# Delta attention, squared-ReLU layer and maxout layer on one core: due places and weights of the written-out schedule changed

## The chip, the cores and the metric

The kernel runs on one core of a Trainium2 chip. The metric is the device time of one execution in microseconds (us); smaller is better. TensorE (PE) multiplies matrices, its weight loads are listed apart as PEld; VectorE (DVE) and ScalarE (ACT) work on tiles, GpSimd (POOL) only fills memory here, and SyncE (SP) issues every DMA, one after the other.

## The reference

Three layers follow each other. The first is a delta-rule attention over 4 batches, 8 heads, 768 steps and head width 48:

```python
for t in range(S):
    kt, vt, bt = (k_n[:, :, t], v[:, :, t], beta[:, :, t, None])
    y[:, :, t] = np.einsum('bhd,bhde->bhe', q[:, :, t], state)
    v_old = np.einsum('bhde,bhd->bhe', state, kt)
    state = state + bt[:, :, :, None] * np.einsum('bhd,bhe->bhde', kt, vt - v_old)
...
h = x @ w_in; g = np.maximum(h, 0) ** 2; x = g @ w_out                     # 384 -> 2048 -> 384
h = np.maximum(np.maximum(x @ w1, x @ w2), x @ w3); return h @ w_out2      # 384 -> 768 -> 384
```

`k_n` is k divided by its norm. Layers two and three work on 3072 rows. The weights arrive as 64-bit floats.

## The kernel before

**Tiling.** The 768 steps are cut into six segments t = 0 to 5 of 128 steps, and each segment into two halves of 64. For each segment there are four pieces of attention work. `gram(t)` (line 499) transposes keys and queries on TensorE and multiplies them; ScalarE and VectorE (with the mask, tile W) move the products. `solve(t)` (line 568) inverts triangular 32x32 blocks on VectorE: a prologue, then 31 steps j of two instructions each (tiles tmp and T, line 621), then transposes (Tn, G) and small TensorE products between them (tiles Tn, G and L). `values(t)` scales v (tile vn). `chain(t)` (line 708) carries the state through the segment: removals (VectorE, tile R), updates (ScalarE, US), states (VectorE, US) and outputs (ScalarE, Y), each with TensorE products in two groups; `rows` (line 792) then issues ten small DMAs, xr<-Y, for each half. The chain needs the solve of its own segment and the state of the chain before it. `split` (line 827) cuts the outputs into a high and a low part, xh and xl.

**The first dense layer.** `moe1(t)` (line 872) works on the 512 rows of segment t in 16 feature blocks f. For each f, `hidden` does 9 matmuls of 512 columns from xh, xl, wih and wil, then squares on ScalarE (r, gh) and VectorE (gl), and `project` does 9 more with wo into three accumulators that stay for the whole segment. At t = 0 the weights of each f are loaded and converted from 64 bits: `load_in` and `load_out`, both by `load_w` (line 839), two ScalarE and seven VectorE instructions apiece, 32 such conversions. The converted wo is written to DRAM (wod<-wo) and streamed back for t > 0 (wo<-wod) into a ring of four buffers (line 426). There is one xh and one xl, so `split(t+1)` waits for the last `hidden` of t. At t = 0 the first eight blocks run in two halves.

**The maxout layer** follows in three planned stages: the rest of moe1 for t = 4 and 5 with the conversions of the maxout weights, then the maxout work.

**What sets the order.** Nothing is issued at once. Each instruction is recorded with a due place `pl.at` (in ticks; one feature block of moe1 is 6 ticks, a segment TICKS = 96) and a modelled cost, and `Planner.issue` writes out an order for all engines together (three calls: lines 996, 1070, 1084). It runs `forward` eight times (line 262): a list schedule in which each engine takes, among the instructions that are ready, the one with the smallest due place. After each round `backward` replaces all due places by the latest places that the schedule just made would allow. The round with the earliest modelled end is issued. So the due places in the code steer the first round, and the later ones through it. On TensorE the dense matmuls (float32r) and the attention's (float32) are two kinds; five weights decide when it goes from one kind to the other (lines 159 to 172): MIX and FULL are the planner's floors of work in a stretch below which it takes dense matmuls, STAY says how much more urgent dense work must be to end a group of attention work, URGENT how much more urgent attention work must be to break into dense work, and BURST how many microseconds of ready attention work break in without being urgent. HOLD (line 150) lets VectorE take an instruction that becomes ready up to so many microseconds after it is free.

**Due places** that the change touches: `solve(1, G1 - TICKS)` (line 979), `chain(t + 1, TICKS * t - CL)` and its values (lines 985, 986), `gram` and `solve` of t + 2 at TICKS * t - GL and 12 later (lines 988, 989), the streamed wo at SPL ticks ahead of its `project` (line 908), and the second half of the small products in solve(0), LATE ticks after the first (lines 664, 691). DEC, BOOST, G2 and the rest stay. chain(0) is due at -192 ticks, and the conversions of block f at 6f - 100 and 6f - 91 (3f in the halves).

Of the kernel before, what the change touches and what calls it, by code (L numbers as in the profile page):

```python
# [52 lines left out]
class Planner:  # L53
# [3 lines left out]

    MIX, FULL, STAY, BURST, URGENT = 4344, 6200, 5.0, 1.5, 5.0  # L60
    INTO, BACK = 0.09, 0.2
    HOLD = {"vector": 0.15}
    LAG = {"tensor": 0.2, "vector": 0.13, "scalar": 0.15, "gpsimd": 0.08, "sync": 0.0}

    def __init__(self, nc):
# [48 lines left out]
    def forward(self, at):  # L114
# [20 lines left out]
        while todo:  # L135
# [13 lines left out]
            r = ready.get(e, [])  # L149
            while r and r[0][0] <= t + self.HOLD.get(e, 0.0):  # L150
                when, n = heappop(r)
# [174 lines left out]
def kernel(  # L326
# [41 lines left out]
    GB = B // 2  # L368
    EPS = 1e-6

    GL, CL, G1, DEC, BOOST, SPL, CUT, HALF, G2, LATE, EARLY = 46, 20, -19, 100, 125, 23, 6, 8, -111, 88, 0
    TICKS = 6 * NF
    W_MIN, W_MAX = 2.0 ** -15, 122876.0

# [740 lines left out]
```

## Time and profile before

| what | value |
|---|---|
| median of three runs | 993.63 us (993.24 to 993.89) |
| the profiled execution | 994.74 us; its span from first to last instruction 992.6 us |
| PE busy | 918.2 us, 92% of the span |
| DVE busy | 581.6 us, 59% |
| ACT busy | 466.8 us, 47% |
| mean granted TensorE clock | 0.942 of full |

How to read it: a busy share is of the whole span, while each stretch has its own limit. The page cuts the span into 40 slices of 24.8 us and gives each engine one digit for each, the tenths in which it was busy, and PEclk the tenths of TensorE's full clock that were granted. TensorE knows two levels here, 2.4 GHz (9, 1.00) and 1.2 GHz (5, 0.5); values between them are slices with both. Matmuls overlap in the records, so a matmul's mean duration is longer than the distance between two starts.

### The profile page before, as it was taken

To read this page: it belongs to the slowest core of one execution; us is meant where nothing else is said; L and a number is where in the kernel's file an instruction comes from. 1 tells how busy PE (TensorE), PEld (TensorE's weight loads), DVE (VectorE), ACT (ScalarE), POOL (GpSimd) and SP (SyncE) were. 2 spreads that over 40 slices of the span, in tenths; PEclk is the share of its full clock that TensorE was granted. 3 is DMA by queue.
4 is the path that set the end of the run, shared out by engine and by line. 5 is a ranking of instruction groups with operands and counts; after the bars stand their busy time and mean duration, and the time that the engine had idled before them with its cause. 6 is when DMAs were issued, how large, how long until landed. Compare 5 with 4: busy or idle time off the path is not lost.

```text
span 992.6 us, 22500 instructions
## 1 busy us (share of the span) xinstructions
PE 918.2 (92%) x9484; PEld 765.7 (77%) x9484; DVE 581.6 (59%) x1240; ACT 466.8 (47%) x853; POOL 21.5 (2%) x29
## 2 busy tenths in 40 slices
PE   6285889978998999999999999999999999999998
PEld 5174778756786888788877778888888888888887
DVE  4999999997249726945962228889532323232221
ACT  6173668635573666367455446766221212222121
POOL 2000000000000000000000000000000000000000
PEclk9556789978998999999999999999999999999999
DMA  9443588454554357425522245765110100000000
GB/s 159 69 124 99 145 255 203 101 159 111 141 105 102 97 138 120 121 78 111 151 88 81 81 145 176 236 186 165 48 46 19 48 17 17 17 17 17 17 17 32
DMA packets 160549, 100.64 MB, mean 101 GB/s; under 512 B 124353, under 2 KB 140481, under 8 KB 160449
## 3 DMA queue, kind: packets, MB, share of 16 engines
q1 hardware_dynamic: 160448, 99.22, 37.8%
q8 instruction: 74, 1.21, 0.5%
q14 instruction: 27, 0.21, 0.1%
HBM read 79.53 MB, written 14.94 MB: 95 GB/s over the span
## 4 chain that ended last, share of the span: by engine, by line
PE 75%; DVE 19%; ACT 2%; issue 2%; DMA 1%; SPq 0%; DVEq 0%; ACTq 0%
PE ps L320 75%; DVE xs L320 4%; DVE tmp L320 3%; DVE T L320 3%; DVE t L320 2%; DVE L L320 1%; DVE W L320 1%; DVE st L320 1%; DVE gl L320 1%; DVE US L320 1%; DVE wo L320 1%; ACT W L320 1%; DVE wil L320 1%; ACT G L320 1%; ACT xs L320 0%
## 5 line engine op out<-in xcount | busy, mean ns | idle before, releaser
L320 PE MATMUL ps<-gh,wo 128*128 128x512 f32 (+1 forms) x624 | 162.2, 390 | 6.7 <-DVE wo L320 4.0
L320 ACT ACTIVATE r<-ps 128x512 f32<-128x512 f32 (+1 forms) x140 | 80.1, 572 | 154.5 <-PE ps L320 140.6
L320 DVE TENSOR_TENSOR r<-r,ps 128x512 f32<-128x512 f32 x72 | 49.5, 688 | 171.8 <-PE ps L320 171.8
L320 PEld LDWEIGHTS ps<-gh,wo 128*128 128x128 f32 x624 | 113.6, 193 | 33.5 <-DVE wo L320 5.1
L320 PE MATMUL ps<-xh,wih 128*128 128x512 f32 (+1 forms) x312 | 126.4, 405 | 6.1 <-ACT wih L320 3.6
L320 PE MATMUL ps<-xh,wil 128*128 128x512 f32 (+1 forms) x312 | 121.7, 390 | 2.8 <-DVE wil L320 2.8
L320 PE MATMUL ps<-xl,wih 128*128 128x512 f32 (+1 forms) x312 | 121.0, 388 | 0.9 <-issue 0.9
L320 DVE TENSOR_TENSOR gl<-r,gh 128x512 fp32r<-128x512 f32 (+1 forms) x104 | 67.2, 646 | 88.0 <-ACT gh L320 81.1
L320 PE MATMUL ps<-gl,wo 128*128 128x512 f32 (+1 forms) x312 | 87.5, 389 | 6.0 <-DVE gl L320 6.0
L320 PEld LDWEIGHTS ps<-xh,wih 128*128 128x128 f32 x312 | 61.1, 196 | 21.1 <-ACT r L320 4.6
L320 PEld LDWEIGHTS ps<-xh,wil 128*128 128x128 f32 x312 | 61.5, 197 | 14.6 <-DVE wil L320 3.8
L320 PEld LDWEIGHTS ps<-xl,wih 128*128 128x128 f32 x312 | 61.5, 197 | 13.6 <-issue 1.3
L320 PEld LDWEIGHTS ps<-gl,wo 128*128 128x128 f32 x312 | 56.9, 192 | 19.6 <-DVE gl L320 7.5
L320 DVE TENSOR_TENSOR T<-T,tmp 128x31 f32<-128x31 f32 (+15 forms) x186 | 63.4, 341 | 4.4
L320 DVE TENSOR_TENSOR tmp<-L,T 128x31 f32<-128x31 f32 (+15 forms) x186 | 63.2, 340 | 4.2
L320 ACT ACTIVATE gh<-r 128x512 fp32r<-128x512 f32 (+1 forms) x104 | 62.0, 596 | 6.1 <-PE ps L320 3.7
L320 ACT ACTIVATE r<-r 128x512 f32<-128x512 f32 (+1 forms) x104 | 62.1, 597 | 2.7
L320 ACT ACTIVATE W<-ps 64x512 f32<-64x512 f32 (+1 forms) x72 | 41.3, 589 | 34.4 <-PE ps L320 33.6
L320 ACT ACTIVATE G<-ps 32x256 f32<-32x256 f32 (+2 forms) x96 | 46.2, 483 | 21.6 <-PE ps L320 20.2
L320 DVE TENSOR_SCALAR xs<-xs 128x384 f32<-128x384 f32 (+1 forms) x112 | 41.4, 372 | 16.1 <-ACT xs L320 14.9
L320 PEld LDWEIGHTS ps<-W 64*64 64x64 f32 x1536 | 36.2, 156 | 14.3 <-ACT W L320 8.5
L320 PE MATMUL ps<-W 64*64 64x64 f32 x1536 | 41.2, 245 | 5.9 <-ACT W L320 5.8
(143 smaller groups left out, 1672.4 us busy)
## 6 DMA issues: line engine op xcount, KB each, us to landing
wo<-wod SPq DMA_DIRECT2D x88, 384.0 KB, 3.2
raw<-in_moe_w_out_dram SPq DMA_DIRECT2D x22, 384.0 KB, 3.6
raw<-in_moe_w_dram SPq DMA_DIRECT2D x18, 384.0 KB, 3.8
raw<-in_moe_w_in_dram SPq DMA_DIRECT2D x16, 384.0 KB, 4.0
wod<-wo SPq DMA_DIRECT2D x16, 384.0 KB, 3.9
vn<-in_v_dram SPq DMA_DIRECT2D x24, 192.0 KB, 4.7
kn<-in_k_dram SPq DMA_DIRECT2D x24, 192.0 KB, 4.6
out_dram<-ob SPq DMA_DIRECT2D x24, 192.0 KB, 1.9
```

The source lines that it names most:

```text
L320: self.plan.add(self.name, lambda: fn(*args, **kw), cost, [out], ins, flow, late)
```

## The change

Ten numbers of the schedule change; no instruction is added or taken away. The weights of the planner: MIX, STAY and URGENT become smaller, BURST larger, and HOLD falls from 0.15 to 0.06 us. The due places: solve(1) becomes due 31 ticks later (G1 -19 to 12), solve and gram of t + 2 three ticks later (GL 46 to 43), chain and values of t + 1 13 ticks earlier (CL 20 to 33), the streamed wo 12 ticks earlier (SPL 23 to 35), and the second half of solve(0)'s products 16 ticks later (LATE 88 to 104).

```diff
-    MIX, FULL, STAY, BURST, URGENT = 4344, 6200, 5.0, 1.5, 5.0
+    MIX, FULL, STAY, BURST, URGENT = 3761.69, 6200, 3.58, 2.57, 3.56
     INTO, BACK = 0.09, 0.2
-    HOLD = {"vector": 0.15}
+    HOLD = {"vector": 0.06}
...
-    GL, CL, G1, DEC, BOOST, SPL, CUT, HALF, G2, LATE, EARLY = 46, 20, -19, 100, 125, 23, 6, 8, -111, 88, 0
+    GL, CL, G1, DEC, BOOST, SPL, CUT, HALF, G2, LATE, EARLY = 43, 33, 12, 100, 125, 35, 6, 8, -111, 104, 0
```

## Rows read from the trace of the kernel before

**Rows 1.** The page's 40 slices: busy tenths of PE and DVE, granted clock.
```profile
PE   6285889978998999999999999999999999999998
...
DVE  4999999997249726945962228889532323232221
...
PEclk9556789978998999999999999999999999999999
```
**Rows 2.** Windows by stretch: length, busy us of each engine (instructions), clock, DMA.
```profile
50.00:108.00 58.00, 41.65 (x891) 36.35 (x886) 56.36 (x127) 31.92 (x62) 3.00 (x3) 0.56 0.50 129
108.00:235.00 127.00, 108.95 (x1503) 90.88 (x1501) 123.53 (x316) 79.28 (x167) 2.88 (x3) 0.90 0.59 164
235.00:320.00 85.00, 80.44 (x1248) 65.38 (x1243) 44.41 (x89) 48.13 (x85) 2.88 (x3) 0.92 0.47 113
320.00:595.00 275.00, 270.15 (x3686) 217.88 (x3685) 148.28 (x300) 156.50 (x272) 5.74 (x6) 1.00 0.43 111
...
183.00:235.00 52.00, 40.44 (x458) 30.07 (x458) 51.28 (x143) 21.71 (x42) 1.92 (x2) 0.84 0.43 121
```
**Rows 3.** Groups by line of DVE, 183 to 235 us: busy us, mean ns.
```profile
L320 DVE TENSOR_TENSOR T<-T,tmp 128x31 f32<-128x31 f32 (+15 forms) x31 | 10.4, 335 | 0.1
...
L320 DVE TENSOR_SCALAR xs<-xs 128x384 f32<-128x384 f32 (+1 forms) x16 | 5.6, 352 | 0.0
L320 DVE SCALAR_TENSOR_TENSOR t<-raw,t 128x384 f32<-128x384 uint32 x8 | 4.4, 549 | 0.0
...
L320 DVE TENSOR_SCALAR t<-xs 128x384 uint32<-128x384 uint32 x8 | 2.8, 351 | 0.0
L320 DVE TENSOR_TENSOR wo<-xs,wo 128x384 fp32r<-128x384 f32 x5 | 2.8, 552 | 0.1
```
**Rows 4.** Timeline of all engines, 74 to 87 us: start, us, idle before.
```profile
81.18 1.22 DVE L320 TENSOR_TENSOR L<-L,st 128x1024 f32<-128x1024 f32 x1
...
86.71 0.44 PE L320 MATMUL ps<-US,W 64*64 64x48 f32 x2 [7.34 <-DVE US L320]
```
**Rows 5.** Timeline of PE and SP: moe1(0) ends, moe1(1) begins, chain rows leave.
```profile
237.59 7.42 SPq L320 DMA_DIRECT2D xr<-Y  x10
...
240.57 0.86 PE L320 MATMUL ps<-gl,wo 128*128 128x512 f32 x3
...
245.78 0.76 PE L320 MATMUL ps<-xh,wih 128*128 128x512 f32 x1
```
**Rows 6.** Window of the stretch in which moe1(1) begins.
```profile
245.00:253.00 8.00, 7.52 (x77) 5.72 (x78) 1.94 (x3) 3.41 (x6) 0.00 (x0) 0.57 0.77 203
```
**Rows 7.** Waits of PE, 105 to 235 us: us in total, times, longest.
```profile
PE ps L320 <- DVE wo L320: 4.0, 2, 2.3
PE ps L320 <- ACT wih L320: 3.6, 1, 3.6
```
**Rows 8.** Waits of PE, 235 to 595 us.
```profile
PE ps L320 <- ACT r L320: 1.4, 2, 0.7
PE ps L320 <- DMA wo<-wod: 0.3, 1, 0.3
```
**Rows 9.** Timeline of PE: one change of kind and back.
```profile
451.46 0.49 PE L320 MATMUL ps<-ident,kt 128*128 128x128 f32 x3
...
452.91 0.96 PE L320 MATMUL ps<-gl,wo 128*128 128x512 f32 x3
```
**Rows 10.** Timelines of PE and DVE: solve(1)'s last products, chain(1)'s first removal.
```profile
154.66 0.37 PE L320 MATMUL ps<-G,L 32*32 32x32 f32 x10
...
164.63 0.55 DVE L320 TENSOR_TENSOR R<-vn,ps 128x384 f32<-128x384 f32 x1
```
**Rows 11.** Timelines of DVE and ACT: first removal and last output of chain(5).
```profile
545.19 0.55 DVE L320 TENSOR_TENSOR R<-vn,ps 128x384 f32<-128x384 f32 x1 [3.21 <-PE ps L320]
...
577.09 0.60 ACT L320 ACTIVATE Y<-ps 112x512 f32<-112x512 f32 x1 [0.28 <-PE ps L320]
```
**Rows 12.** Waits of SP's queue, 105 to 595 us: total, times, longest.
```profile
SPq L320 <- PE ps L320: 207.7, 86, 7.3
```

## The prediction, made before the changed kernel was run

> **What bounds the kernel now.** I read the 40 slices of the page first [rows 1]. Three stages show. In the first nine or ten slices DVE stands at 9 while PE has digits between 2 and 9 and PEclk between 5 and 9; in the middle PE stands at 9 with a few 8s; in the last sixteen slices PE is full at the full clock and DVE sinks to 2 or 3. The windows put numbers to it [rows 2]. From 50 to 108 us DVE is busy 56.36 of 58 us and PE 41.65, at 0.56 of its clock. From 108 to 235 us, in which moe1(0) runs at the pace of its converted weights, DVE is busy 123.53 of 127 us. From 320 us PE is busy 270.15 of 275 us at clock 1.00. So up to 235 us VectorE sets the pace, behind that TensorE, and the reordering has room only in the first stage and where the two meet.
>
> What DVE does ahead of 235 us is read from its groups [rows 3]. One conversion is two xs<-xs of 352 ns, three instructions of some 549 ns (t<-raw stands for them), one t<-xs of 351 ns and the low part of 552 ns: 2 x 0.352 + 3 x 0.549 + 0.351 + 0.552 = 3.25 us. There are 32, so 104 us, and none can go. In the same stretch stand all 31 steps of solve(2): T takes 10.4 us, and its twin tmp as much, some 21 us that no matmul of moe1(0) needs. In that stretch, 183 to 235 us, PE is busy 40.44 of 52 us at 0.84 of the clock [rows 2].
>
> **The change part by part.** No instruction is added or removed on any engine or queue; each one keeps its duration, and only places change. Every term is therefore idle or half-clock time of PE. A due place reaches the chip only through the planner, so none of the terms is sure.
>
> 1. *solve(1) 31 ticks later, LATE 16 later.* At 86.71 us PE ends a wait of 7.34 us for chain(0)'s state, while DVE works on solve(1)'s prologue (L<-L,st at 81.18) [rows 4]. With solve(1) due later the state goes first. At most the 7.34 us are won; at least nothing, because the conversions' end at 235 us follows from DVE's sum, which the order leaves alone. I take 1 us, near the low end, since DVE has only 127 - 123.53 = 3.47 us to spare there [rows 2]. Solve(0)'s second half of products, LATE later, hides in PE's 58 - 41.65 = 16.4 us of idle time in the same stretch [rows 2]; without that cover it would delay chain(0)'s second half by its own length. What is late next is the conversion, on which PE waited 3.6 us (wih) and 4.0 us (wo) [rows 7].
>
> 2. *chain(1) 13 ticks earlier.* moe1(0) ends with the matmuls at 240.57, chain(1)'s last rows leave SP only from 237.59 on (7.42 us for ten DMAs), and the first matmul of moe1(1) starts at 245.78 [rows 5]. In the 8 us from 245 to 253 PE is at 0.57 of the clock and idle 0.48 us [rows 6]. If the chain ends ahead of moe1(0), the loss 8 x 0.43 + 0.48 = 3.9 us goes, and that is the upper end. The lower end is a loss: DVE instructions of the chain that are pulled in front of the last conversion, at 0.55 us each, some four of them, 2.2 us. I take a gain of 2.5 us. The SP queue carries the same ten issues, earlier.
>
> 3. *gram and solve of t + 2 three ticks later.* Three ticks are half a feature block, so about one conversion goes in front of work of solve(2): 0 to 3.25 us [rows 3]. I take 1 us. For t of 3 and up it costs nothing, since DVE is busy 148.28 of 275 us there [rows 2].
>
> 4. *HOLD.* DVE's idle time ahead of 235 us is 1.64 + 3.47 = 5.1 us [rows 2], the most that a shorter hold could give. Against it, an urgent instruction that comes just behind the shorter hold waits behind one of about 0.55 us [rows 3]; with eight such cases on PE's path that would cost 4.4 us. I take a gain of 1 us.
>
> 5. *BURST, URGENT, STAY, MIX.* One turn to attention work and back reads 452.91 - 451.46 = 1.45 us for three transposes and 32 small products [rows 9]; the turn itself is no more than 0.2 us of it, an estimate from the 0.1 us or so by which the matmuls at its two ends start late. With some 40 such groups from 235 to 595 us (counted along the timeline), a quarter fewer give 2 us. From below, one more stretch like that at 245 us costs 3.9 us [rows 6]. I take 1 us.
>
> 6. *Streamed wo 12 ticks earlier.* All that PE lost for it behind 235 us is 0.3 us for the DMA itself and 1.4 us where two hidden blocks follow each other and wait for r [rows 8]: 0 to 1.7 us, and I take 0.5. What would be late next on SP is a rival, below.
>
> The sum is 1 + 2.5 + 1 + 1 + 1 + 0.5 = 7.0 us. The profiled execution took 994.74 us (span 992.6 and 2.1 around it), so 987.7; the median of the runs lies 1.1 us lower, so **986.6 us**.
>
> **Rivals.** *Slower: solve(1) too late for chain(1).* Its last products start at 154.66, and chain(1) begins with its removal at 164.63 [rows 10], so some 10 us are free. Moe1(0) makes 96 ticks in the 133 us from 108 to 241, 1.38 us a tick; 31 ticks are 43 us, and solve(1) would end near 198. A chain alone needs 577.09 + 0.6 - 545.19 = 32.5 us [rows 11], which leads to 230.5, still ahead of the 237.59 at which the last rows leave now. But in the DVE-bound stage chain(1) took 73 us, from 164.63 to 237.59. The rival decides where the chain keeps a pace of over 40 us: at 50 us it ends at 248, 10 us late, and moe1(1) with it. Due places speak for it, as solve(1) moves 31 ticks back while its chain moves 13 forward; the backward rounds speak against it, since they give solve(1) the place that its chain needs. Time: 993.6 + 10 = 1003.6 us.
>
> *Much faster: solve(2) slides behind the conversions.* Then some 21 us of steps leave the bound stretch [rows 3]; PE loses there 52 x (1 - 0.84) = 8.3 us by its clock and 11.6 us idle [rows 2], so a gain of about 16 us: 977.6. For it speaks that chain(2) needs solve(2) only after moe1(1) has begun; against it that its due place moves three ticks only.
>
> *No difference.* Eight rounds replace the due places, and the round kept may end in much the same order, with gains and losses of 1 us: 993.6.
>
> *Slower through SP.* The wo ring has four buffers, which is 24 ticks of blocks, and 35 ticks ahead asks for more. A wo load that stands at the head of SP's queue waits until PE frees a buffer, and the ten xr<-Y behind it wait as well. SP already waited 207.7 us for PE in 86 waits, 2.4 us each [rows 12]; one at each of the four changes of segment t = 1 to 4 makes 9.7 us: 1003.3. Against it: the planner puts a load on the queue only when its buffer is free in the model. The Trainium skill, DMA: Bandwidth & Descriptors, section Anatomy of one DMA, has the rule that a semaphore wait is done by the issuing sequencer before dispatch and never by the DMA engines; by that rule this rival's queue would stand. The trace agrees so far that SP itself shows the waits.
>
> **How the numbers follow.** The forecast gets 0.47, solve(2) behind the conversions 0.12, no difference 0.12, solve(1) too late 0.23, SP 0.06. What a measurement of this kernel can tell from no change is about 0.2%, 2 us. Faster by more is 0.47 + 0.12 = 0.59, within it 0.12, slower 0.23 + 0.06 = 0.29. The likeliest case alone reaches from 981 to 991.5, with two or three terms at their better or worse ends. The range for all takes in both the strong gain and the two losses: 976 to 1004.
>
> **What would show it.** In the changed profile the wait for US near 87 us should be gone, chain(1)'s last xr<-Y should leave ahead of the last gl,wo of moe1(0), and the low clock near 245 us should shrink. The last conversion should end at about 233 to 235 us if term 1 is right that DVE's sum holds it, and well ahead of it if solve(2) has moved. The forecast is wrong if moe1(1) starts later than 246 us, if PE's idle time behind 320 us grows over 5 us, or if xr<-Y stands behind wo<-wod in SP's queue.

## The result and the profile after

The changed kernel takes 961.23 us in the median (960.95 to 962.98) against 993.43 us for the kernel before beside it: a ratio of 0.968 (95% interval 0.966 to 0.970), 32 us or 3.2% faster. The forecast was faster, with 986.6 us and a range from 976 to 1004. The direction held; the gain is over four times the one forecast, and the time lies outside the range.

The page's slices of the kernel after, to be read against [rows 1]:

```profile
PE   6437899999999999999999999999999999999998
...
DVE  5999998999479469459713389893323232322221
...
PEclk9556799999999999999999999999999999999999
```

A slice is 24.0 us long here. PE reads 7 and 8 in the fourth and fifth slices and 9 from the sixth on, and PEclk reads 6 and 7 there and then 9; before, both were still uneven in slices nine, ten and thirteen. DVE is about as full in the first slices as it was.

To say where the 33.7 us of the two spans went, both spans are cut at the same points of the work: at 108 us, at the last gl,wo of moe1(0) and at the last gl,wo of moe1(4). The windows of the kernel before (length, busy us of PE, PEld, DVE, ACT, POOL, clock, DMA):

```profile
0.00:108.00 108.00, 64.52 (x1241) 55.24 (x1243) 90.45 (x223) 50.00 (x96) 9.97 (x17) 0.64 0.59 122
108.00:241.40 133.40, 115.35 (x1647) 96.24 (x1643) 128.26 (x321) 83.59 (x174) 3.84 (x4) 0.91 0.58 160
241.40:628.20 386.80, 377.39 (x4923) 304.61 (x4923) 216.28 (x441) 221.82 (x392) 7.67 (x8) 0.98 0.46 118
628.20:992.60 364.40, 360.92 (x1684) 309.65 (x1682) 146.66 (x258) 111.43 (x194) 0.00 (x0) 1.00 0.17 56
```

and of the kernel after:

```profile
0.00:108.00 108.00, 62.41 (x1180) 52.18 (x1181) 93.76 (x246) 54.03 (x104) 9.76 (x17) 0.65 0.65 138
108.00:220.00 112.00, 107.56 (x1628) 90.58 (x1629) 106.99 (x260) 78.83 (x163) 2.99 (x3) 0.98 0.66 175
220.00:594.40 374.40, 370.25 (x4997) 300.30 (x4996) 237.86 (x505) 226.82 (x401) 8.60 (x9) 1.00 0.48 126
594.40:958.90 364.50, 360.92 (x1684) 309.63 (x1682) 134.94 (x232) 105.83 (x187) 0.00 (x0) 1.00 0.16 52
```

The stage of moe1(0) is 21.4 us shorter, the one up to the end of moe1(4) 12.4 us, and the rest is unchanged. For each stage two losses of PE can be read: its idle time (length less busy) and its clock loss (length times one less the clock). In moe1(0) the idle time goes from 18.1 to 4.4 us and the clock loss from 12.0 to 2.2 us; in the next stage from 9.4 to 4.2 and from 7.7 to 0. Up to 108 us neither moves by more than about 2 us.

This account holds for the whole span and for all seventeen kernels of this study. Before, PE was idle 992.6 - 918.2 = 74.4 us, and lost 992.6 x (1 - 0.942) = 57.6 us by its clock; after, 57.8 and 39.3 us. The span less these two sums is 860.6 and 861.8 us, and between 854 and 866 us for every other kernel. TensorE's work is fixed, and the reordering moves the 132 us of the two losses, now 97. The account is good to some 6 us and not to one.

### The profile page after: what moved, and what is told of

The parts are those of the page before. It is cut to its first block, busy times and chain, and to the rows that moved or that the text cites. A ratio compares the mean times of both kernels' runs of the same rounds, so it can differ in the third digit from the quotient of the medians.

```text
span 958.9 us, 22535 instructions
## 1 busy us (share of the span) xinstructions
PE 901.1 (94%) x9484; PEld 752.7 (78%) x9484; DVE 573.5 (60%) x1240; ACT 465.5 (49%) x853; POOL 21.4 (2%) x29
## 3 DMA queue, kind: packets, MB, share of 16 engines
q1 hardware_dynamic: 160448, 99.22, 39.3%
## 4 chain that ended last, share of the span: by engine, by line
PE 80%; DVE 14%; ACT 3%; issue 1%; DMA 1%; SPq 0%; POOL 0%; DVEq 0%; ACTq 0%; POOLq 0%
PE ps L320 80%; DVE xs L320 3%; DVE tmp L320 2%; DVE T L320 2%; DVE W L320 2%; DVE t L320 1%; ACT G L320 1%; DVE L L320 1%; DVE US L320 1%; DVE wo L320 0%; DVE gl L320 0%; DMA raw<-in_moe_w_in_dram 0%; DVE st L320 0%; SPq L320 0%; ACT W L320 0%
## 5 line engine op out<-in xcount | busy, mean ns | idle before, releaser
L320 PEld LDWEIGHTS ps<-gh,wo 128*128 128x128 f32 x624 | 111.3, 190 | 28.9 <-ACT gh L320 1.8
L320 PE MATMUL ps<-xh,wih 128*128 128x512 f32 (+1 forms) x312 | 123.7, 397 | 2.2 <-ACT r L320 1.5
L320 PE MATMUL ps<-xh,wil 128*128 128x512 f32 (+1 forms) x312 | 119.1, 382 | 0.0
L320 PE MATMUL ps<-gl,wo 128*128 128x512 f32 (+1 forms) x312 | 85.3, 382 | 0.0
L320 PEld LDWEIGHTS ps<-xh,wih 128*128 128x128 f32 x312 | 59.5, 191 | 16.1 <-ACT r L320 2.3
L320 PEld LDWEIGHTS ps<-xl,wih 128*128 128x128 f32 x312 | 59.5, 191 | 14.1 <-DVE xl L320 2.0
L320 ACT ACTIVATE G<-ps 32x256 f32<-32x256 f32 (+2 forms) x96 | 46.3, 483 | 13.8 <-PE ps L320 12.3
L320 PE MATMUL ps<-W 64*64 64x64 f32 x1536 | 42.4, 244 | 9.6 <-ACT W L320 9.3
L320 ACT ACTIVATE W<-ps 64x512 f32<-64x512 f32 (+1 forms) x72 | 41.4, 590 | 17.6 <-PE ps L320 16.1
```

What stands on the lines that cost most here:

```text
L320: self.plan.add(self.name, lambda: fn(*args, **kw), cost, [out], ins, flow, late)
```

## The experiments

HOLD, the number that the forecast gave 1 us, turned out to be the change. The planner puts 0.13 us (LAG of VectorE, line 63) behind a VectorE instruction before another one that depends on it is ready. At HOLD 0.15 the next step of a solve counts as ready when the step before it ends; at 0.06 it does not, and any other instruction that is ready goes in between. I call this theory A; B holds the due places for the cause, C TensorE's weights. In the table, the ratios are to the kernel before, run beside each (992.6 to 994.0 us); idle and clock loss are as above, of the profiled execution. The last column gives, of the same execution, when moe1(0) ends and how long it is from there to the end of moe1(4), both at the last gl,wo; what follows takes 364.4 or 364.5 us in every kernel.

| run | edit to the kernel before | median us | ratio (95%) | idle + clock loss us | end of moe1(0) + on to moe1(4) us |
|---|---|---|---|---|---|
| before | | 993.4 | | 74.4 + 57.6 | 241.4 + 386.8 |
| after | all ten numbers | 961.2 | 0.968 (0.966 to 0.970) | 57.8 + 39.3 | 220.0 + 374.4 |
| e1 | HOLD 0.06 | 962.7 | 0.972 (0.969 to 0.974) | 56.6 + 43.2 | 225.1 + 370.9 |
| e2 | all but HOLD | 977.3 | 0.986 (0.983 to 0.989) | 69.4 + 45.8 | 229.0 + 381.8 |
| e3 | the five due places | 985.6 | 0.994 (0.992 to 0.997) | 78.0 + 44.2 | 226.9 + 391.0 |
| e4 | the four weights of TensorE | 993.7 | 1.001 (0.999 to 1.003) | 73.5 + 53.5 | 239.7 + 386.6 |
| e5 | HOLD 0.12 | 975.8 | 0.980 (0.975 to 0.985) | 64.8 + 44.7 | 229.2 + 378.6 |
| e6 | HOLD 0.14 | 996.2 | 1.002 (1.000 to 1.004) | 79.2 + 60.6 | 245.1 + 384.3 |
| e7 | 0.06 for the solves' steps alone | 977.9 | 0.983 (0.979 to 0.987) | 63.6 + 46.7 | 226.1 + 381.8 |
| e8 | 0.06 for all but the steps | 980.2 | 0.985 (0.982 to 0.989) | 69.0 + 49.8 | 242.0 + 370.8 |
| e9 | 0.06 for the steps of solve(0) to (2) | 986.5 | 0.994 (0.991 to 0.996) | 68.3 + 58.3 | 231.5 + 392.4 |
| e10 | LAG of VectorE 0.16, HOLD 0.15 | 973.0 | 0.979 (0.976 to 0.982) | 68.5 + 40.8 | 229.0 + 377.6 |
| e11 | HOLD 0 | 968.2 | 0.974 (0.971 to 0.977) | 60.5 + 42.4 | 227.3 + 372.2 |
| e12 | all but G1 | 968.7 | 0.974 (0.970 to 0.977) | 65.5 + 44.6 | 230.9 + 374.4 |
| e13 | HOLD off while gl stands ready | 990.5 | 0.996 (0.995 to 0.998) | 71.6 + 58.3 | 245.3 + 378.8 |
| e14 | HOLD off while a conversion stands ready | 984.8 | 0.991 (0.988 to 0.993) | 69.3 + 48.2 | 228.3 + 390.8 |
| e15 | HOLD off while either stands ready | 977.7 | 0.984 (0.982 to 0.986) | 64.8 + 43.8 | 229.2 + 379.6 |

**Which part of the change: e1 to e4.** The first takes HOLD alone:

```diff
-    HOLD = {"vector": 0.15}
+    HOLD = {"vector": 0.06}
```

> The kernel before with HOLD 0.06 alone. Theory A (HOLD: below the 0.13 us that the planner puts between dependent VectorE instructions, the solve's steps no longer run back to back; conversions come between, and the last conversion ends earlier): 962 to 974 us, last wo conversion near 220 us instead of 235. Theory B (due places of solve(1) and chain(1) did it): 988 to 996 us. Theory C (TensorE's weights did it): 988 to 996 us.

962.67 us: 30 of the 32 us, as theory A has it. The second is the changed kernel with this one line turned back.

> The changed kernel with HOLD back at 0.15. Theory A: most of the gain goes, 982 to 994 us; if the due places move the solve behind the conversions as well, half of it, 970 to 980. Theory B and C: 960 to 966 us.

977.33 us, in the band of "half of it". So the other nine numbers are worth 15 us while HOLD is 0.15, and only 1.4 us on top of HOLD 0.06 (962.67 against 961.23 us, measured at different times and too close to tell apart). The gains do not add up. The third has the line of the due places alone (GL, CL, G1, SPL, LATE).

> The kernel before with the five due places alone (G1, CL, GL, SPL, LATE). Its VectorE order has 143 of solve steps' instructions ahead of the last conversion instead of 186, but as many back to back (73). Theory A: 980 to 994 us. Theory B: 961 to 970 us. If what counts is only how many steps stand ahead of the last conversion, at 0.25 to 0.34 us each: 11 to 15 us gained there, 978 to 983 us.

985.55 us, 7 us gained, in the band of theory A and short of the 11 to 15 us of the step count. The last wo conversion came 12.3 us earlier (222.8 instead of 235.1 us), and yet the time fell by 7 only: idle time of PE rose from 74.4 to 78.0 us, and only the clock loss fell. By stage, moe1(0) ended 14.5 us earlier and the next stage took 4.2 us more. How early the conversions end is therefore not the whole yardstick. The fourth has MIX, STAY, BURST and URGENT alone.

> The kernel before with MIX, STAY, BURST and URGENT alone. Theory A and B: 990 to 997 us, since the VectorE order ahead of the last conversion stays (186 steps, 67 back to back). Theory C: 961 to 975 us.

993.71 us, no difference: theory C falls.

**Is it the 0.13 us: e5, e6, e10, e11.** HOLD 0.12 and 0.14 differ by two hundredths.

> The kernel before with HOLD 0.12, just under the 0.13 us that the planner puts between dependent VectorE instructions. Theory A (it matters on which side of 0.13 HOLD lies): 964 to 976 us, as with 0.06; its VectorE order has 12 back-to-back pairs of solve steps ahead of the last conversion where the kernel before has 74, and 165 steps instead of 186. Theory D (the gain grows with every hundredth of HOLD): 983 us, a third of the way from 0.15 to 0.06.

> The kernel before with HOLD 0.14, just above 0.13. Theory A: 988 to 997 us, no gain (70 back-to-back pairs, 185 steps). Theory D: 989 us, a ninth of the way.

975.84 and 996.21 us. The gain does not grow with the hundredths; it jumps by 20 us between 0.12 and 0.14, and theory D falls. e5 lies at the upper edge of its band, 13 us slower than e1, so under the step something still varies. The cross-check leaves HOLD at 0.15 and raises the other time over it:

```diff
-    LAG = {"tensor": 0.2, "vector": 0.13, "scalar": 0.15, "gpsimd": 0.08, "sync": 0.0}
+    LAG = {"tensor": 0.2, "vector": 0.16, "scalar": 0.15, "gpsimd": 0.08, "sync": 0.0}
```

> The kernel before with HOLD left at 0.15, and the time that the planner puts behind a VectorE instruction raised from 0.13 to 0.16 us, so that HOLD lies under it. Theory A (the side on which HOLD lies of that time): 962 to 978 us. Theory E (a small HOLD is good by itself, the other time has no part in it): 988 to 998 us.

972.95 us. HOLD was left large and the gain came, so theory E falls. A larger LAG also keeps other instructions behind VectorE longer, which this run does not separate; with e5 and e6, where LAG stayed, it shows that what counts is on which side of LAG HOLD lies. The last of this group has HOLD 0:

> The kernel before with HOLD 0. Theory A: gains as 0.06 and 0.12 do, 962 to 977 us; which of the two ends it comes near tells how much the planner's own scatter does. Theory E: the smallest hold is the fastest, under 962 us.

968.24 us. Under the step, 0, 0.06 and 0.12 give 968, 963 and 976: a scatter of 13 us in no order, which I put down to the planner ending in another order each time; no run tests that. It is also the measure for what follows: a difference of less than 13 us between two orders can be the planner's.

**Who was held, and who waited: e7, e8, e9.** A set marks the tmp and T instructions of the solves, and line 150 is split:

```diff
-            while r and r[0][0] <= t + self.HOLD.get(e, 0.0):
+            while r and r[0][0] <= t + (0.0 if e != "vector" else self.STEP if r[0][1] in self.steps else self.OTHER):
```

e7 has STEP 0.06 and OTHER 0.15, e8 the opposite.

> The kernel before with HOLD 0.15 for all of VectorE's instructions but the solves' 31 steps, which get 0.06. Theory A in its narrow form (the solves' steps alone do it, since only they hold VectorE for tens of instructions): 960 to 972 us. Rival: the hold matters for the conversions, masks and gl as well: 975 to 990 us.

> The opposite: 0.15 for the solves' steps alone, 0.06 for all else. Theory A in its narrow form: 984 to 997 us (83 back-to-back pairs, 171 steps ahead of the last conversion). Rival: 962 to 978 us.

977.89 us lies in the rival's band, 980.18 us between the two bands. The narrow form of theory A falls: the solves' steps make 16 us of the gain and the hold on the other instructions 14, together the 30 us of e1. The windows of moe1(0) from 108 us on, and of the stage behind it, show where each lies. First e7, then e8:

```profile
108.00:226.10 118.10, 105.01 (x1499) 89.30 (x1498) 110.49 (x273) 77.75 (x162) 3.00 (x3) 0.94 0.60 163
226.10:607.90 381.80, 375.91 (x5067) 304.16 (x5066) 231.15 (x484) 226.31 (x399) 8.62 (x9) 1.00 0.47 123
```

```profile
108.00:242.00 134.00, 112.10 (x1565) 94.06 (x1566) 124.89 (x316) 85.54 (x174) 2.86 (x3) 0.91 0.62 175
242.00:612.80 370.80, 368.72 (x5016) 298.46 (x5015) 229.09 (x479) 223.96 (x397) 8.61 (x9) 1.00 0.48 124
```

Up to the end of moe1(0), e1 gains 16.3 us on the kernel before, e7 15.3, and e8 loses 0.6; from there to the end of moe1(4), e1 gains 15.9, e7 5.0 and e8 16.0. So ahead of that end the hold on the solves' steps costs the time, and behind it mostly the hold on the other instructions. In the four runs under the step (e1, e5, e10, e11) the first of these lengths varies by 4 us and the second by 8, so the scatter does not make these differences. e9 is e7 with the mark only for t < 3.

> As the run with the solves' steps free (0.06) and 0.15 for all else, but only the steps of solve(0) to solve(2) are free; those of solve(3) to solve(5) are held by 0.15 again. If the gain of the free steps (about 16 us) lies in the DVE-bound stage: 975 to 982 us. If it lies behind it, where a held solve keeps gl waiting: 985 to 993 us.

986.52 us, in the band of "behind it". By the medians the early solves make 6.5 us and the late ones the other 9 to 10, but that is less than the scatter of 13 us, so the time alone does not show it. Nor do the stages quite: the profiled execution of e9 is the slowest of its seven (990.39 us), that of e7 the fastest of its four (974.43), and of the 16 us between them 5.4 stand ahead of the end of moe1(0), where the steps are free in both. The other 10.6 stand behind it, where they differ. The waits of PE behind 222 us show what the late solves stood in the way of there (us in total, times, longest). First e9, where solve(3) to solve(5) are held, then e7, where they are free:

```profile
PE ps L324 <- DVE gl L324: 6.7, 2, 3.7
```

```profile
PE ps L324 <- issue: 3.5, 4, 1.4
```

The wait for gl is gone in e7; the line shown is its longest. In e8, where the steps are held, it is only 0.2 us too, so a held step alone does not make gl wait. The timeline of the kernel before shows how it came about (start, us, engine):

```profile
304.58 0.63 ACT L320 ACTIVATE gh<-r 128x512 fp32r<-128x512 f32 x1
...
310.74 0.69 DVE L320 TENSOR_TENSOR gl<-r,gh 128x512 fp32r<-128x512 f32 x1
...
311.48 1.65 PE L320 MATMUL ps<-gl,wo 128*128 128x512 f32 x3 [2.98 <-DVE gl L320]
```

gh is there at 305.21, gl starts at 310.74, and between them VectorE does nothing but solve(3)'s steps. PE idles for 2.98 us. The windows ahead of 310.7 us and behind it show the clock fall to its lower level, 1.2 GHz:

```profile
300.00:310.70 10.70, 8.50 (x64) 6.60 (x62) 9.74 (x30) 4.10 (x7) 1.29 (x2) 1.00 0.37 98
```

```profile
310.70:317.50 6.80, 6.03 (x14) 4.77 (x15) 6.42 (x16) 1.86 (x3) 0.00 (x0) 0.50 0.44 112
```

In the kernel after, in the middle of the same solve:

```profile
285.86 0.63 ACT L320 ACTIVATE gh<-r 128x512 fp32r<-128x512 f32 x1
...
286.52 0.69 DVE L320 TENSOR_TENSOR gl<-r,gh 128x512 fp32r<-128x512 f32 x1
...
290.98 0.66 PEld L320 LDWEIGHTS ps<-gl,wo 128*128 128x128 f32 x3
```

gl starts 0.03 us after gh ends, and its weight loads begin at 290.98 us, 3.8 us after gl ends, without a wait.

**Whose turn it should have been: e13, e14, e15.** Here HOLD stays 0.15 and is dropped only while an instruction of a marked kind stands ready on VectorE: gl in e13, those of the weight conversions in e14, both in e15.

```diff
-            while r and r[0][0] <= t + self.HOLD.get(e, 0.0):
+            while r and r[0][0] <= t + (0.0 if any(x[1] in self.meek for x in q) else self.HOLD.get(e, 0.0)):
```

> The kernel before with HOLD 0.15, which is dropped only while a gl instruction stands ready on VectorE. Theory F (behind the conversions, the gain is that gl no longer stands behind a held solve): the waits of PE for gl after 235 us, 5.3 us, go, with the low clock behind them; 982 to 989 us. Rival: the solves' other victims matter there (W masks, chain): 990 to 997 us.

> The kernel before with HOLD 0.15, which is dropped only while an instruction of a weight conversion stands ready on VectorE. Theory G (ahead of the last conversion, the gain is that conversions fill the places between a solve's steps): 23 back-to-back pairs instead of 74; last wo conversion at 225 to 230 us; gain of 8 to 16 us, 977 to 985 us. Rival (the order ahead of the last conversion does not matter while VectorE is full): 988 to 997 us.

> Both of these: HOLD 0.15 dropped while a gl or a conversion stands ready. Theories F and G together: 965 to 977 us, near the kernel with HOLD 0.06. If something else in the small hold matters as much: 978 to 988 us.

990.47, 984.79 and 977.68 us. gl alone missed its band by 1.5 us: PE's waits for gl went, but others came, for US and G (2.2 and 1.5 us). By stage, e13 gains 8.0 us behind the end of moe1(0), where theory F has its gain, and loses 3.9 ahead of it, both about as much as the scatter there. The conversions gave 9 us, with the last wo at 224.4 us: 13.1 gained ahead of that end and 4.0 lost behind it. Both gave 16 us (12.2 and 7.2 by stage), just between the two bands, and as much as freeing the solves' steps. The other 14 us of e1 lie with the hold on further instructions, by stage mostly behind moe1(0); which ones, no run here tells.

**One due place: e12**, the changed kernel with G1 at -19.

> The changed kernel with solve(1) due where it was before (G1 -19). If the later solve(1) brings nothing once HOLD is small: 958 to 966 us, the same as the changed kernel. If it brings what the due places alone brought (7 us): 966 to 970 us. Its VectorE order has 3 back-to-back pairs and 158 steps ahead of the last conversion, the changed kernel 14 and 145.

968.69 us, in the second band, so the later solve(1) is worth 7.5 us in the changed kernel. That is within the scatter of 13 us seen between neighbouring values of HOLD, and e1 reaches 962.67 us with G1 at -19. I don't read a cause into it. LATE and SPL do nothing here: with either turned back, the changed kernel's issued order is the same on every engine. No run beat the changed kernel.

## Why the forecast was right in direction and wrong in size

**Term 4, HOLD, is the step that failed.** I priced it by VectorE's idle time ahead of 235 us, "the most that a shorter hold could give", and took 1 us of 5.1. HOLD alone gave 30 us. The idle time was the wrong quantity: at 0.15 VectorE was not idling, it was serving the wrong instruction. (The 5.1 us are also only those from 50 to 235 us; the first 50 us have another 15.9.) The two numbers 0.15 and 0.13 stand on neighbouring lines of the code (62 and 63), and that the new HOLD falls under LAG could be seen there. That the direction held is in part luck, since most of the gain came by a way that no term names.

**"the reordering has room only in the first stage and where the two meet"** failed as well. Between the ends of moe1(0) and moe1(4) the kernel before had 9.4 us of PE's idle time and 7.7 of clock loss, and 12.4 of the 33.7 us came from there, in e1 15.9. VectorE was only 56% busy there (216.28 of 386.8 us), and still kept PE waiting for gl. (The reading of the slices was off too, though nothing hung on it: DVE does not sink to 2 or 3 in all of the last sixteen, whose first four read 8, 8, 8 and 9.)

**"The conversions' end at 235 us follows from DVE's sum, which the order leaves alone"** (term 1) failed too. The last wo conversion now ends at 217.1 us, not at the 233 to 235 of the forecast's test. The groups of DVE up to that point, in the kernel before (0 to 234.5 us) and after (0 to 217.6 us), show what left the sum:

```profile
L320 DVE TENSOR_TENSOR T<-T,tmp 128x31 f32<-128x31 f32 (+15 forms) x93 | 31.5, 339 | 1.4
L320 DVE TENSOR_TENSOR tmp<-L,T 128x31 f32<-128x31 f32 (+15 forms) x93 | 31.4, 338 | 1.3
```

```profile
L320 DVE TENSOR_TENSOR T<-T,tmp 128x31 f32<-128x31 f32 (+15 forms) x73 | 24.0, 329 | 0.3
L320 DVE TENSOR_TENSOR tmp<-L,T 128x31 f32<-128x31 f32 (+15 forms) x73 | 24.0, 329 | 0.4
```

Three whole solves (93 steps) stood ahead of it before; after, two and eleven steps of the third. This is the rival "solve(2) slides behind the conversions", for two thirds of its steps, and it needed no due place: in e1 the last conversion is at 220.5 us with GL and G1 unchanged. The rival had the right place and a chance of only 0.12, because I looked only at the three ticks of its due place. Its price of 16 us is near the 16.3 by which moe1(0) ends earlier in e1, but its own two numbers, 8.3 and 11.6, add up to 19.9, so that is in part luck. It is not the only thing: in e3 the due places alone move 43 step instructions behind the last conversion, and the gain is 7 us.

**The sum is smaller as well, not only reordered.** The steps of a solve depend on each other. The timeline of the kernel before shows two back to back, then that of the kernel after with other work between them:

```profile
309.57 0.39 DVE L320 TENSOR_TENSOR tmp<-L,T 128x220 f32<-128x220 f32 x1
310.00 0.39 DVE L320 TENSOR_TENSOR T<-T,tmp 128x220 f32<-128x220 f32 x1
```

```profile
211.27 0.35 DVE L320 TENSOR_SCALAR xs<-xs 128x384 f32<-128x384 f32 x1
211.54 0.35 DVE L320 TENSOR_TENSOR tmp<-L,T 128x192 f32<-128x192 f32 x1
211.81 0.55 DVE L320 TENSOR_TENSOR wo<-xs,wo 128x384 fp32r<-128x384 f32 x1
212.28 0.35 DVE L320 TENSOR_TENSOR T<-T,tmp 128x192 f32<-128x192 f32 x1
```

Behind a step that it needs, the next one starts 0.04 us after the end in the record; between unrelated instructions the next starts 0.08 us before the end (211.54 against 211.27 + 0.35). Each back-to-back pair that is split saves some 0.12 us. Ahead of the last conversion the timeline has 74 such pairs before and 14 after, so 60 x 0.12 = 7.2 us; the 40 or so step instructions that moved behind make 40 x (0.33 - 0.08) = 10 us. Together 17 us of the 18 us by which the conversions end earlier. That a pair costs this is read from the trace; no run priced it alone, and e7, with no pair left ahead of the last conversion, is slower than e1 with 21. Nor is it a rule for other orders: in e12, 71 pairs and 28 step instructions fewer make 15 us by the same count, and the last conversion ends 6.4 us earlier, because VectorE idles 8 us more ahead of it.

**Terms 2 and 1.** moe1(1) starts ahead of moe1(0)'s end, as term 2 wanted: its first matmul stands at 214.84 us and the last gl,wo of moe1(0) at 219.15, and PEclk shows no dip there. Term 2 was sized 2.5 us with 3.9 at the upper end; the clock loss of all the stretch from 108 us to moe1(0)'s end fell by 9.8 us. CL was neither needed for it nor enough: e1 has the same with CL at 20 (218.64 against 224.26 us), and in e3, with CL at 33 and HOLD 0.15, moe1(1) starts behind that end (229.54 against 225.95). What CL adds beside a small HOLD isn't shown. In term 1, chain(0)'s wait for US did not go, it shrank, from 7.34 to 2.83 us. Up to 108 us PE's waits for W on VectorE fell too, from 16.1 us in one to 9.4 in three, but those for G on ScalarE rose from 0.4 to 10.7. The longest wait for W and the one for US, in PE's timeline of the kernel after:

```profile
68.78 1.11 PE L320 MATMUL ps<-ident,qt 128*128 128x128 f32 x4 [5.21 <-DVE W L320]
...
95.89 0.31 PE L320 MATMUL ps<-US,W 64*64 64x48 f32 x2 [2.83 <-DVE US L320]
```

PE's idle time up to 108 us is 45.6 us, before 43.5. So 1 us was high rather than low there.

**Term 3** (three ticks, 1 us) was run only together with the other due places (e2, e3), so its share is open. **Term 6** (SPL) gave nothing, since the issued order of the changed kernel is the same without it. **Term 5** (TensorE's weights, 1 us) can't be told from 0 by e4, whose interval holds 1 us as well.

**The rivals on the slower side.** solve(1) was not too late for its chain: its last products went from [rows 10] 154.66 to 162.02 us, not to the 198 of that rival. SP did wait for PE as before (228.3 us in 84 waits from 105 to 595 us, [rows 12] 207.7 in 86), and chain(1)'s last xr<-Y left from 208.71 us on, 29 us earlier than in [rows 5]; that rival did not come.

**The range.** Each of the six terms was bounded by the idle time or the clock at one place. The pool from which any reordering draws, 74.4 us of idle time and 57.6 us of lost clock, stood on the first page and would have set a far higher upper end; some 35 of these 132 us were won.

## What to carry to other kernels

Where a written-out schedule has thresholds, compare each new value with the other constants it is compared with in the code: crossing one of them gave 18 to 30 us here (e1, e5, e10, e11), while changes on one side of it moved the time by at most 13 us and in no order. An engine that is full can still be serving the wrong work, so price a rule of choice by whom it keeps waiting and by what that costs the engine that bounds, not by the idle time of the engine itself. For an upper end, add the bounding engine's idle time and its clock loss over the span before summing places.

## What the runs showed of the hardware

A dependent VectorE instruction directly behind its producer cost some 0.12 us more than the same instruction with unrelated work between. The Trainium skill, VectorE: DVE Perf Modes, section The DRAIN you can't avoid, says that a next op starts only when the pipe is empty, that one which is not held starts earlier, and that in its measurement a semaphore after each op cost nothing extra. This trace agrees that unrelated neighbours start earlier, 0.08 us before the recorded end; a step that waits for the one before it starts 0.04 us after that end, so here the wait does cost something, and the measurement decides.

The lost clock was worth as much as the idle time. The wait of 2.98 us for gl was followed by 6.03 busy us at half the clock, which cost another 3.0 us (an estimate: half of the 6.03). Over the whole span the clock loss fell by 18.3 us and the idle time by 16.6 us.
